# Second GEMM half a batch behind the first, in a Nystrom-attention and squared-ReLU kernel

## Chip, cores, metric

One core of a Trainium2 chip. The metric is device time in microseconds (us) of one execution, median of several. A ratio is the mean time of one kernel's fast runs over the mean of the other's in the same rounds, so it is not quite the ratio of the medians quoted. On one core, executions come in a state "fast" unless they are over 1.5% above the fastest of the same kernel.

Names: PE is TensorE (PEld its weight loads), DVE is VectorE, ACT is ScalarE, POOL is GpSimd, SP is SyncE. A "q" behind a name means its instruction queue, as in SPq.

## The reference, cut

```python
# B, H, S, D = 8, 8, 576, 64;  m = 32 landmarks;  d_model 512, d_ff 2048
q_lm, k_lm = segment means of q and k            # 32 segments of 18 rows
A, Bm, C = softmax(q k_lm^T/8), softmax(q_lm k_lm^T/8), softmax(q_lm k^T/8)
Z = Bm^T / (norm1(Bm) * norminf(Bm) + 1e-6)
for _ in range(6): Z = 2*Z - Z @ Bm @ Z          # Newton steps
x = (A @ Z @ C @ v) as [4608, 512]
h = relu(x @ w_in);  out = (h*h) @ w_out         # first GEMM, second GEMM
```

## The kernel before: what the argument touches

The eight batches run as a software pipeline: while batch b goes through the first GEMM, attention of batch b+1 is interleaved, and the second GEMM works on batch b-1. A list scheduler reorders instructions of each engine by priority, so the program order is a wish, not the final order. Each engine then executes its own queue in order.

Loads come in through GpSimd's queue and are cast to bf16. Tails are the last 64 rows of q and k:

```python
def load_qk(b, X):
    X["qkt"] = loads.tile([P, H, D], BF16, tag="qkt", name="qkt")
    for nm, src, r0 in (("k", k, TAIL), ("q", q, 0)):
        raw = loads.tile([P, H, NC4, D], BF16, tag="raw", name="raw")
        nc.gpsimd.dma_start(raw[:], ...)                       # bulk of k, then of q
        nc.gpsimd.dma_start(X["qkt"][r0:r0 + TAIL, :, :], ...) # its tail
```

VectorE then copies each into another layout, and from batch 2 on a transposing DMA issued by SyncE makes the transposed form:

```python
def prepare(b):
    for nm in ("k", "q"):
        X[nm] = loads.tile(..., tag=nm + "nat", bufs=1, name="nat")
        nc.vector.tensor_copy(X[nm][:], X[nm + "raw"]...)      # waits for the load
        if b >= 2:
            nc.sync.dma_start_transpose(X[nm + "T"]..., X[nm]...)
```

First GEMM, second GEMM and the loop:

```python
def mlp_in(b, f, AT, G, gT):           # 16 f-blocks a batch
    h = psum.tile([P, 2, 512], F32, tag="h", bufs=2, name="h")
    ... 4 matmuls of 288 columns
    nc.scalar.activation(r..., h[:, :, 0:HALF], AF.Relu)
    nc.vector.tensor_tensor(gT[:, f, o:o + S], r[:], r[:], ALU.mult)

def mlp_out(b, gT):                    # 9 tiles in two batches, 16 matmuls each
    for t in ...:
        ops = psum.tile([P, DM], F32, tag="o", bufs=1, name="ops")
        ... 16 matmuls of 512 columns, a yield after each
        o_sb = mlp.tile([P, DM], F32, tag="o", name="o_sb")    # two buffers
        if t % 2: nc.scalar.copy(o_sb[:], ops)
        else:     nc.vector.tensor_copy(o_sb[:], ops)
        nc.sync.dma_start(out_rows, o_sb[:])                   # store by SyncE

for b in range(B):
    load_qk(b + 2, ...); load_v(b + 2, ...)
    att, tiles = attention(b + 1, R), mlp_out(b - 1, prev)
    for u in range(2 * NF):
        if u % 2 == 0: mlp_in(b, u // 2, AT, G, gT)
        else:          advance(tiles, per)
        advance(att, ...)
        if u == NF and b + 2 < B: prepare(b + 2)
    ...
```

The softmax here doesn't subtract the row's maximum and nothing guards it: scores larger than these inputs give would overflow.

## Time and profile before

Median 315.67 us (315.25 to 315.75, 4 runs).

The view of the stages, kernel before: for each stretch of time its length, then the busy time of each engine in it with the number of instructions, the granted TensorE clock, the DMA share and what DMA moved.

```profile
0.00:40.00 40.00, 20.87 (x262) 15.20 (x263) 23.15 (x67) 12.96 (x30) 22.10 (x39) 0.83 1.28 176
40.00:60.00 20.00, 16.08 (x163) 11.92 (x162) 13.31 (x37) 13.86 (x26) 3.81 (x5) 0.83 1.52 163
60.00:80.00 20.00, 13.55 (x145) 7.62 (x144) 13.69 (x32) 6.58 (x13) 4.68 (x6) 0.88 1.44 170
80.00:100.00 20.00, 18.98 (x174) 12.15 (x172) 16.53 (x41) 12.59 (x26) 1.56 (x2) 0.95 1.01 129
100.00:180.00 80.00, 78.17 (x753) 45.26 (x752) 58.28 (x134) 44.08 (x82) 13.13 (x16) 1.00 0.85 121
```

The first busy figure is TensorE's. From 100 us on it is busy 98% of the time; the idle time lies in the first 100 us.

The waits of TensorE from 38 to 104 us, kernel before (who waited for whom, total us, times, longest us), the three longest:

```profile
PE h L419 <- DVE G L410: 5.4, 2, 5.1
PE n L353 <- DVE st L242: 3.8, 1, 3.8
PE n L368 <- ACT U L356: 0.8, 2, 0.5
```

Two waits make up nearly all of it, and both are for VectorE. The waits of VectorE from 38 to 80 us, kernel before, say what VectorE stood at:

```profile
DVE nat L156 <- DMA T<-nat: 5.1, 1, 5.1
DVE nat L156 <- DMA raw<-in_k_dram: 3.8, 1, 3.8
```

And VectorE's instructions in order of time around both, kernel before (start, us, instruction, in brackets the idle time ahead of it and what ended it):

```profile
48.69 0.69 DVE L156 COPY nat<-raw 128x2048 bf16<-128x2048 bf16 x1 [3.83 <-DMA raw<-in_k_dram]
49.30 0.75 DVE L242 TENSOR_TENSOR st<-BS,blk 128x256 bf16<-128x256 f32 x2
...
75.03 0.70 DVE L156 COPY nat<-raw 128x2048 bf16<-128x2048 bf16 x1 [5.09 <-DMA T<-nat]
75.76 1.23 DVE L410 CAST G<-g 128x1024 bf16<-128x1024 f32 x1
```

Read it like this: at 44.9 us VectorE reached the copy of a coming batch's k whose load had not landed. Behind it in the queue stood the start of batch 1's Newton steps (line 242), which had all its inputs. The Trainium skill, "PSUM — Partial Sum Buffer", section "Engine vs sequencer instructions", says that these queues are strict FIFO; this trace agrees, at 3.83 and 5.09 us each. The second time the copy waited until the transposing DMA had read its single buffer.

**A measure used below.** Busy time hides small gaps and the clock, so I also count work: each weight load in a stretch stands for one matmul, and each kind gets its spacing back to back as this trace shows it (216 ns in the second GEMM, 122 ns in the first, 25 to 134 ns for the small ones). The stretch less that sum is "lost time". It is an estimate. Its level hangs on the spacings taken for the small matmuls, so read only the differences between kernels; they are good to about 1 us a stretch.

### The profile page before, as it was taken

The page shows a single profiled execution, that of the slowest core. Times are in us where ns is not written, and L with a number is a line of the kernel's source. Part 1 is how long each engine was busy: PE and PEld are TensorE (multiplying, and loading weights), DVE is VectorE, ACT ScalarE, POOL GpSimd, SP SyncE. Part 2 cuts the span into 40 slices and gives each one's busy share as a digit, 9 for nine tenths or more (in the row PEclk, how much of TensorE's full clock was granted, in tenths as well). Part 3 has the DMA queues.
Part 4 walks back from the last instruction along what each step waited for, and adds up shares of the span by engine and source line. Part 5 has one row for each costly group of instructions (what it writes and reads, how often), then busy time and mean ns, then how long its engine had stood idle before and what let it go on. Part 6 is the DMA issues. An engine that isn't in the chain of part 4 may idle for free.

```text
span 315.4 us, 6319 instructions
## 1 busy us (share of the span) xinstructions
PE 276.1 (88%) x2536; PEld 164.8 (52%) x2536; DVE 201.4 (64%) x473; ACT 154.3 (49%) x291; POOL 46.9 (15%) x70
## 2 busy tenths in 40 slices
PE   0376786983998999999999999999989999999994
PEld 0264455642664566555655566466635665555441
DVE  3358765984797577768785858677964686544010
ACT  1053474731764466446744574448534754555000
POOL 8733513121010300104010401000000000000000
PEclk9995695997799999999999999999999999999999
DMA  8999999999967399819982996563000101000131
GB/s 90 186 198 201 203 198 167 127 174 168 176 87 110 88 124 176 125 70 142 154 143 72 138 144 148 82 123 83 33 35 34 35 35 67 33 35 33 67 102 67
DMA packets 75358, 35.28 MB, mean 112 GB/s; under 512 B 42049, under 2 KB 70721, under 8 KB 75329
## 3 DMA queue, kind: packets, MB, share of 16 engines
q0 software_dynamic: 41856, 18.35, 48.5%
q1 hardware_dynamic: 33472, 16.52, 27.8%
q8 instruction: 20, 0.33, 0.5%
q14 instruction: 10, 0.07, 0.1%
HBM read 36.70 MB, written 9.44 MB: 146 GB/s over the span
## 4 chain that ended last, share of the span: by engine, by line
PE 63%; DMA 18%; DVE 8%; ACT 5%; issue 4%; POOL 2%; DVEq 0%; POOLq 0%; ACTq 0%
PE ops L435 31%; PE h L419 15%; DMA T<-nat 6%; DMA w_in_bf<-in_moe_w_in_dram 5%; DMA raw<-in_k_dram 4%; DMA vm<-in_v_dram 3%; ACT r L423 3%; PE g L402 2%; PE n L279 2%; PE n L329 2%; PE n L353 2%; DVE gT L424 2%; PE n L368 1%; DVE ra L306 1%; PE n L177 1%
## 5 line engine op out<-in xcount | busy, mean ns | idle before, releaser
L435 PE MATMUL ops<-w_out_bf,gT 128*128 128x512 bf16 x544 | 145.4, 380 | 3.3 <-DVE o_sb L443 1.6
L423 ACT ACTIVATE r<-h 128x576 bf16<-128x576 f32 x128 | 82.9, 654 | 69.0 <-PE h L419 53.2
L419 PE MATMUL h<-AT,G 128*128 128x288 bf16 x512 | 87.4, 294 | 6.0 <-DVE G L410 5.4
L424 DVE TENSOR_TENSOR gT<-r 128x576 bf16<-128x576 bf16 x128 | 57.0, 449 | 40.3 <-ACT r L423 39.8
L435 PEld LDWEIGHTS <-gT 128*128 128x128 bf16 x576 | 51.7, 98 | 44.9 <-issue 7.5
L419 PEld LDWEIGHTS <-G 128*128 128x128 bf16 x512 | 48.0, 100 | 27.4 <-issue 8.4
L356 ACT CAST U<-n 128x256 bf16<-128x256 f32 (+1 forms) x54 | 18.7, 353 | 20.6 <-PE n L353 20.4
L408 ACT CAST G<-g 128x1024 bf16<-128x1024 f32 x16 | 16.2, 1012 | 21.9 <-PE g L402 21.8
L443 DVE COPY o_sb<-ops 128x512 f32<-128x512 f32 x20 | 13.7, 685 | 20.2 <-PE ops L435 20.2
L410 DVE CAST G<-g 128x1024 bf16<-128x1024 f32 x16 | 19.6, 1225 | 10.8 <-PE g L402 10.7
L156 DVE COPY nat<-raw 128x2048 bf16<-128x2048 bf16 x16 | 11.2, 700 | 17.9 <-DMA raw<-in_k_dram 7.7
L370 DVE SCALAR_TENSOR_TENSOR st<-st,n 128x256 bf16<-128x256 bf16 (+1 forms) x45 | 17.0, 386 | 8.2 <-PE n L368 7.0
L353 PE MATMUL n<-st,BT 128*128 128x128 bf16 x96 | 14.4, 228 | 6.4 <-DVE st L242 3.8
L177 PE MATMUL n<-seg,nat 128*128 128x32 bf16 x256 | 11.3, 180 | 8.4 <-DVE nat L156 8.4
L375 DVE STREAM_TRANSPOSE st<-st 128x256 bf16<-128x256 bf16 (+1 forms) x45 | 17.8, 402 | 0.6
L84 POOL DMA_DIRECT2D vm<-in_v_dram x8 | 7.1, 884 | 71.1 <-PE n L331 69.5
L353 PEld LDWEIGHTS <-BT 128*128 128x128 bf16 x96 | 8.8, 101 | 16.0 <-DVE st L242 4.3
L177 PEld LDWEIGHTS <-nat 128*128 128x128 bf16 x256 | 10.3, 98 | 11.7 <-DVE nat L156 8.6
L73 POOL DMA_DIRECT2D raw<-in_k_dram x8 | 8.0, 1003 | 55.8 <-DVE nat L156 55.0
L279 PEld LDWEIGHTS <-T 128*128 128x128 bf16 x256 | 12.0, 102 | 2.9 <-issue 2.2
L402 PE MATMUL g<-w_in_bf,WT 64*32 64x512 bf16 x256 | 12.4, 412 | 0.7 <-ACT G L408 0.5
L306 DVE TENSOR_REDUCE ra<-EA 128x40 f32<-128x1280 f32 x8 | 11.8, 1475 | 1.4 <-ACT EA L295 1.1
(153 smaller groups left out, 307.1 us busy)
## 6 DMA issues: line engine op xcount, KB each, us to landing
out_dram<-o_sb SPq DMA_DIRECT2D x32, 256.0 KB, 2.4
raw<-in_k_dram POOLq DMA_DIRECT2D x8, 512.0 KB, 11.9
raw<-in_q_dram POOLq DMA_DIRECT2D x8, 512.0 KB, 14.1
vm<-in_v_dram POOLq DMA_DIRECT2D x8, 512.0 KB, 8.1
w_in_bf<-in_moe_w_in_dram POOLq DMA_DIRECT2D x4, 512.0 KB, 12.7
w_out_bf<-in_moe_w_out_dram POOLq DMA_DIRECT2D x4, 512.0 KB, 16.8
out_dram<-o_sb SPq DMA_DIRECT2D x8, 128.0 KB, 6.0
qkt<-in_k_dram POOLq DMA_DIRECT2D x8, 64.0 KB, 12.3
```

The source lines that it names most:

```text
L177: nc.tensor.matmul(means[:, ti, p, :], lhsT=src.rearrange("p h d -> p (h d)"), rhs=seg[:, c + (ti if c == NC4 else 0), :], start=(c == 0), ...
L279: nc.tensor.matmul(sc[:, :, c, j, :] if nm == "q" else sc[:, c, j, :, :], lhsT=X[nm + "T"][:, c, p, :], rhs=BD[:, 1 if nm == "q" else 0, p ...
L353: nc.tensor.matmul(nu[:, qd - g[0], :], lhsT=BT[:, qd, :], rhs=st[:, 0, qd, :], start=True, stop=True)
L356: nc.scalar.copy(Ug[:], nu[:])
L370: last = nc.vector.scalar_tensor_tensor(out=res[:, g[0]:g[-1] + 1, :].rearrange("p q n -> p (q n)"), in0=st[:, z, g[0]:g[-1] + 1, :].rearr ...
L375: nc.vector.transpose(stn[:, 1, g[0]:g[-1] + 1, :].rearrange("p q n -> p (q n)"), stn[:, 0, g[0]:g[-1] + 1, :].rearrange("p q n -> p (q n)"))
L402: nc.tensor.matmul(g[M * p:M * p + M, i, :], lhsT=WT[64 * i:64 * i + 64, p, M * i:M * i + M], rhs=w_in_bf[64 * i:64 * i + 64, p, n * 512:n ...
L410: nc.vector.tensor_copy(dst, g[:])
L419: nc.tensor.matmul(h[:, j, 0:HALF], lhsT=G[:, qd, f * P:(f + 1) * P], rhs=AT[:, qd, j * HALF:(j + 1) * HALF], start=(qd == 0), stop=(qd == 1))
L423: nc.scalar.activation(r.rearrange("p (j t) -> p j t", j=2), h[:, :, 0:HALF], AF.Relu)
L424: nc.vector.tensor_tensor(gT[:, f, o:o + S], r[:], r[:], ALU.mult)
L435: nc.tensor.matmul(ops, lhsT=gT[:, f, t * P:t * P + P], rhs=w_out_bf[:, f, :], start=(f == 0), stop=(f == NF - 1))
```

## The change

Its intent: fill the early stages, in which TensorE has little to do but attention's latency chain, with the second GEMM of the same batch; keep VectorE from standing at copies whose data are not there; shorten batch 0's attention, which nothing overlaps; and take outputs off VectorE and SyncE. The core of the diff, cuts marked:

```diff
+DMA_T = 3                                   # transposing DMA only from batch 3 on
 ... load order: w_in 0, 1, then v of batch 0, w_in 2, 3, then q/k of batch 1, w_out, v of batch 1
-            if b >= 2:
+            if b >= DMA_T:
                 nc.sync.dma_start_transpose(...)
 ... attention of batch 0: prepare(0, ("k",)) and k's means and transposes first, then q;
     transposes in the "h" PSUM; fixed VectorE order; one group instead of two
 ... all batches: BT ahead of the scaling, Newton step 0 from BT; row sums of A in halves;
     the scaling of C v and one copy of A^T on ScalarE; g blocks 2, 3 behind the last output matmul
+            if it == (5 if b < 2 else 1):
+                X["pin"] = last             # this Newton step's update on VectorE
 def mlp_out(b, gT):
-            if b == B - 1 and t % 2:
+            if t % NC4 == 0 and t < 8 or b == B - 1 and t % 2 == 0:
                 ops = psum.tile([P, 2, DM], F32, tag="h", ...)   # the first GEMM's PSUM
-            o_sb = mlp.tile([P, DM], F32, tag="o", name="o_sb")
-            if t % 2: nc.scalar.copy(...)  else: nc.vector.tensor_copy(...)
+            o_sb = mlp.tile([P, DM], F32, tag="o", bufs=3, name="o_sb")
+            nc.scalar.copy(o_sb[:], ops)
-                nc.sync.dma_start(rows[:, c, :], o_sb[:])
+                nc.scalar.dma_start(rows[:, c, :], o_sb[:])
 loop over b:
-        tiles = mlp_out(b - 1, prev)        # in turn with all of mlp_in(b)
-            if u == NF and b + 2 < B: prepare(b + 2)
+        for f in range(NF):
+            mlp_in(b, f, AT, G, gT)
+            advance(tiles, 3 if b % 2 == 0 else 2)
+            attend(...)                     # 60% of attention(b + 1)
+        tiles = mlp_out(b, gT)              # of the same batch
+        for u in range(8):
+            advance(tiles, 3)
+            attend(...)                     # the other 40%
+ in attend, once "pin" of batch b + 1 exists:
+            with tc.issue_after(loaded[b + 1]["pin"].ins): prepare(b + 2)
```

More of the change, by code (lines that the diff above doesn't have):

```diff
@@ L1 @@
-from contextlib import ExitStack
+from contextlib import ExitStack, nullcontext
 import concourse.bass as bass
@@ L115 @@
     nc.vector.memset(ones_bf[:], 1.0)
-    load_v(0, loaded[0])
     def load_w_in(j):
@@ L126 @@
     load_w_in(1)
+    load_v(0, loaded[0])
+    load_w_in(2)
+    load_w_in(3)
     bds = []
@@ L137 @@
     load_qk(1, loaded[1])
-    load_w_in(2)
-    load_w_in(3)
-    load_v(1, loaded[1])
     for j in range(4):
@@ L145, with prepare @@
         )
+    load_v(1, loaded[1])
     def ntile(shape, dt=F32):
         return psum.tile(shape, dt, tag="n", bufs=3, name="n")
-    def prepare(b: int):
+    def prepare(b: int, nms=("k", "q")):
         X = loaded[b]
-        for nm in ("k", "q"):
+        for nm in nms:
             X[nm] = loads.tile([P, NC4, H, D], BF16, tag=nm + "nat", bufs=1, name="nat")
@@ L160, in prepare, with transposes @@
                     X[nm].rearrange("p c h d -> p (c h d)"))
-        X["tT"] = attn.tile([P, NPAIR, P], BF16, tag="tT", name="tT")
-        if b >= 2:
-            nc.sync.dma_start_transpose(X["tT"][:], X["qkt"].rearrange("p h d -> p (h d)"))
+        if "q" in nms:
+            X["tT"] = attn.tile([P, NPAIR, P], BF16, tag="tT", name="tT")
+            if b >= DMA_T:
+                nc.sync.dma_start_transpose(X["tT"][:], X["qkt"].rearrange("p h d -> p (h d)"))
     def attention(b: int, R: dict):
-        X = loaded.pop(b)
+        X = loaded[b]
         BD = bds[b % 2]
         ect = ects[b % 2]
-        groups = [(0,), (1,)] if b == 0 else [(0, 1)]
+        first = b == 0
+        def transposes(nm, half):
+            if first:
+                tps = psum.tile([P, 2, 2, NPAIR, P], BF16, tag="h", bufs=2, name="tps")[:, 0, :, :, :]
+            else:
+                tps = ntile([P, 2, NPAIR, P], BF16)[:]
+            for i in range(2):
+                for p in range(NPAIR):
+                    nc.tensor.transpose(
+                        tps[:, i, p, :],
+                        X[nm][:, 2 * half + i, 2 * p:2 * p + 2, :].rearrange("p h d -> p (h d)"),
+                        ident_bf[:],
+                    )
+            dst = X[nm + "T"][:, 2 * half:2 * half + 2, :, :]
+            if half == 0 and not (first and nm == "q"):
+                nc.vector.tensor_copy(dst, tps)
+            else:
+                nc.scalar.copy(dst, tps)
         means = ntile([P, 2, NPAIR, M])
+        STk = small.tile([P, NPAIR, M], BF16, tag="STk", name="STk")
         for ti, nm in ((1, "k"), (0, "q")):
+            if first:
+                prepare(0, (nm,))
             for p in range(NPAIR):
@@ L182, in attention @@
                     )
-            yield
-        STk = small.tile([P, NPAIR, M], BF16, tag="STk", name="STk")
-        nc.scalar.copy(STk[:], means[:, 1, :, :])
-        nc.scalar.copy(BD[0:64, :, :, 0:M], means[0:64, :, :, :])
-        nc.vector.tensor_copy(BD[64:128, :, :, M:2 * M], means[64:128, :, :, :])
-        def transposes(nm, half):
-            tps = ntile([P, 2, NPAIR, P], BF16)
-            for i in range(2):
-                for p in range(NPAIR):
-                    nc.tensor.transpose(
-                        tps[:, i, p, :],
-                        X[nm][:, 2 * half + i, 2 * p:2 * p + 2, :].rearrange("p h d -> p (h d)"),
-                        ident_bf[:],
-                    )
-            dst = X[nm + "T"][:, 2 * half:2 * half + 2, :, :]
-            if half == 0:
-                nc.vector.tensor_copy(dst, tps[:])
-            else:
-                nc.scalar.copy(dst, tps[:])
+            lo = nc.scalar.copy(BD[0:64, ti, :, 0:M], means[0:64, ti, :, :])
+            hi = nc.vector.tensor_copy(BD[64:128, ti, :, M:2 * M], means[64:128, ti, :, :])
+            tc.declare_no_dep(hi.ins, lo.ins, reason="other partitions")
+            if nm == "k":
+                nc.scalar.copy(STk[:], means[:, 1, :, :])
+                if first:
+                    transposes("k", 0)
+                    transposes("k", 1)
+            yield
         bm = ntile([P, 2, M])
@@ L222, in attention @@
         yield
-        if b < 2:
+        if b < DMA_T:
             transposes("q", 0)
@@ L235, in attention @@
         nc.vector.reciprocal(rc[:], c1[:])
-        BS = small.tile([P, 2, 2, M], F32, tag="BS", name="BS")
-        nc.vector.tensor_tensor(
-            BS[:], BB[:],
-            rc[:, :].unsqueeze(1).unsqueeze(3).to_broadcast([P, 2, 2, M]), ALU.mult)
         def spread(dst, src):
@@ L246, in attention @@
         spread(BT[:], BB[:, 0, :, :])
+        BS = small.tile([P, 2, 2, M], F32, tag="BS", name="BS")
+        nc.vector.tensor_tensor(
+            BS[:], BB[:],
+            rc[:, :].unsqueeze(1).unsqueeze(3).to_broadcast([P, 2, 2, M]), ALU.mult)
         st = newt.tile([P, 2, 2, 4, M], BF16, tag="st", name="st")
-        for z in range(2):
+        for z in (1, 0):
             spread(st[:, z, :, :, :], BS[:, z, :, :])
@@ L252, in attention @@
         yield
-        if b < 2:
+        if b < DMA_T:
             for nm, half in (("q", 1), ("k", 0), ("k", 1)):
-                transposes(nm, half)
-                yield
+                if not first or nm == "q":
+                    transposes(nm, half)
+                    yield
             tps = ntile([P, NPAIR, P], BF16)
@@ L300, in tails, with a_sums, a_rows, a_transposed @@
                 tl[P - TAIL:P, :, 0, :], AF.Exp, scale=SCALE)
-        def a_rows():
-            ea = EA.rearrange("p q c (h m) -> p (q c h) m", m=M)
-            n = 2 * (NC4 + 1) * 4
-            ra = small.tile([P, n], F32, tag="ra", name="ra")
-            nc.vector.reduce_sum(ra[:], ea, axis=AX.X)
-            rra = small.tile([P, n], F32, tag="rra", name="rra")
-            nc.vector.reciprocal(rra[:], ra[:])
-            nc.vector.tensor_tensor(an.rearrange("p q c (h m) -> p (q c h) m", m=M), ea,
-                                    rra[:, :].unsqueeze(2).to_broadcast([P, n, M]), ALU.mult)
-        def a_transposed(qd):
+        rra = [None, None]
+        def a_sums(i):
+            ra = small.tile([P, (NC4 + 1) * 4], F32, tag="ra", name="ra")
+            nc.vector.reduce_sum(ra[:], EA[:, i, :, :].rearrange("p c (h m) -> p (c h) m", m=M),
+                                 axis=AX.X)
+            rra[i] = small.tile([P, (NC4 + 1) * 4], F32, tag="rra", name="rra")
+            nc.vector.reciprocal(rra[i][:], ra[:])
+        def a_rows(i):
+            nc.vector.tensor_tensor(
+                an[:, i, :, :].rearrange("p c (h m) -> p (c h) m", m=M),
+                EA[:, i, :, :].rearrange("p c (h m) -> p (c h) m", m=M),
+                rra[i][:, :].unsqueeze(2).to_broadcast([P, (NC4 + 1) * 4, M]), ALU.mult)
+        def a_transposed(i):
             tps = ntile([P, (NC4 + 1) * P], BF16)
@@ L316, in a_transposed @@
                 o = j * P - (TAIL if b % 2 and j else 0)
-                nc.tensor.transpose(tps[:, o:o + P], an[:, qd, c, :], ident_bf[:])
-            nc.vector.tensor_copy(AT[:, qd, :], tps[:, 0:S])
+                nc.tensor.transpose(tps[:, o:o + P], an[:, i, c, :], ident_bf[:])
+            if i == 0 and not first:
+                nc.vector.tensor_copy(AT[:, i, :], tps[:, 0:S])
+            else:
+                nc.scalar.copy(AT[:, i, :], tps[:, 0:S])
         cvbs = [None, None]
@@ L335, in c_values @@
             cvb = small.tile([P, 4 * D], BF16, tag="cvb", name="cvb")
-            nc.vector.tensor_scalar(out=cvb[:], in0=cv[:, 0:4 * D], scalar1=rc2[:], scalar2=None,
-                                    op0=ALU.mult)
+            nc.scalar.activation(cvb[:], cv[:, 0:4 * D], AF.Copy, scale=rc2[:])
             cvbs[qd] = cvb
-        side = [lambda: scores("q", 0), lambda: scores("q", 1), lambda: scores("k", 0),
-                lambda: scores("k", 1), tails, a_rows, lambda: c_values(0),
-                lambda: c_values(1), lambda: a_transposed(0), lambda: a_transposed(1)]
@@ L345, in attention, with aside @@
-        zt = None
+        side = [(scores, "q", 0), (scores, "q", 1), (tails,), (a_sums, 0, scores, "k", 0),
+                (a_rows, 0, scores, "k", 1), (a_sums, 1, a_transposed, 0),
+                (a_rows, 1, c_values, 0), (a_transposed, 1), (c_values, 1)]
+        def aside():
+            f, *args = side.pop(0)
+            if f in (a_sums, a_rows):
+                f(args[0])
+                f, *args = args[1:]
+            f(*args)
         zt = newt.tile([P, 2, P], BF16, tag="zt", name="zt")
-        U = [None, None]
@@ L348, in attention @@
         for it in range(6):
-            stn = newt.tile([P, 2, 2, P], BF16, tag="st", name="st")
-            for g in groups:
-                nu = ntile([P, len(g), P])
-                for qd in g:
-                    nc.tensor.matmul(nu[:, qd - g[0], :], lhsT=BT[:, qd, :], rhs=st[:, 0, qd, :],
-                                     start=True, stop=True)
-                Ug = newt.tile([P, len(g), P], BF16, tag="U", name="U")
-                nc.scalar.copy(Ug[:], nu[:])
-                for qd in g:
-                    U[qd] = Ug[:, qd - g[0], :]
+            nu = ntile([P, 2, P])
@@ new lines, in attention @@
+            for qd in range(2):
+                nc.tensor.matmul(nu[:, qd, :], lhsT=BT[:, qd, :],
+                                 rhs=st[:, 0, qd, :] if it else BT[:, qd, :],
+                                 start=True, stop=True)
+            U = newt.tile([P, 2, P], BF16, tag="U", name="U")
+            if it:
+                nc.scalar.copy(U[:], nu[:])
+            else:
+                for qd in range(2):
+                    nc.scalar.activation(U[:, qd, :], nu[:, qd, :], AF.Copy, scale=rc[:, qd:qd + 1])
@@ L359, in attention @@
             yield
             if side:
-                side.pop(0)()
+                aside()
                 yield
-            for g in groups:
-                nv = ntile([P, len(g), P])
-                z = 0 if it < 5 else 1
-                for qd in g:
-                    a, c = (st[:, 1, qd, :], U[qd]) if it < 5 else (U[qd], st[:, 1, qd, :])
-                    nc.tensor.matmul(nv[:, qd - g[0], :], lhsT=a, rhs=c, start=True, stop=True)
-                res = stn[:, 0, :, :] if it < 5 else zt[:]
-                last = nc.vector.scalar_tensor_tensor(
-                    out=res[:, g[0]:g[-1] + 1, :].rearrange("p q n -> p (q n)"),
-                    in0=st[:, z, g[0]:g[-1] + 1, :].rearrange("p q n -> p (q n)"), scalar=2.0,
-                    in1=nv.rearrange("p q n -> p (q n)"), op0=ALU.mult, op1=ALU.subtract)
-                if it < 5:
-                    nc.vector.transpose(
-                        stn[:, 1, g[0]:g[-1] + 1, :].rearrange("p q n -> p (q n)"),
-                        stn[:, 0, g[0]:g[-1] + 1, :].rearrange("p q n -> p (q n)"))
@@ L378, in attention @@
-            st = stn
-            if it == 5:
-                X["last"] = last
+            nv = ntile([P, 2, P])
+            for qd in range(2):
+                x, y = (st[:, 1, qd, :], U[:, qd, :]) if it < 5 else (U[:, qd, :], st[:, 1, qd, :])
+                nc.tensor.matmul(nv[:, qd, :], lhsT=x, rhs=y, start=True, stop=True)
+            if it < 5:
+                stn = newt.tile([P, 2, 2, P], BF16, tag="st", name="st")
+                res, old = stn[:, 0, :, :], st[:, 0, :, :]
+            else:
+                res, old = zt[:], st[:, 1, :, :]
@@ L381, in attention @@
+            last = nc.vector.scalar_tensor_tensor(out=res, in0=old, scalar=2.0, in1=nv[:],
+                                                  op0=ALU.mult, op1=ALU.subtract)
+            if it < 5:
+                nc.vector.transpose(stn[:, 1, :, :].rearrange("p q n -> p (q n)"),
+                                    stn[:, 0, :, :].rearrange("p q n -> p (q n)"))
+                st = stn
+            if it == (5 if b < 2 else 1):
+                X["pin"] = last
             yield
             if side:
-                side.pop(0)()
+                aside()
@@ L398, in attention @@
         for n in range(4):
-            g = psum.tile([P, 2, 512], F32, tag="h", bufs=2, name="g")
-            for p in range(NPAIR):
-                for i in range(2):
-                    nc.tensor.matmul(g[M * p:M * p + M, i, :],
-                                     lhsT=WT[64 * i:64 * i + 64, p, M * i:M * i + M],
-                                     rhs=w_in_bf[64 * i:64 * i + 64, p, n * 512:n * 512 + 512],
-                                     start=True, stop=True)
+            with tc.issue_after(mark[0].ins) if n == 2 and mark else nullcontext():
+                g = psum.tile([P, 2, 512], F32, tag="h", bufs=2, name="g")
+                for p in range(NPAIR):
+                    for i in range(2):
+                        nc.tensor.matmul(g[M * p:M * p + M, i, :],
+                                         lhsT=WT[64 * i:64 * i + 64, p, M * i:M * i + M],
+                                         rhs=w_in_bf[64 * i:64 * i + 64, p, n * 512:n * 512 + 512],
+                                         start=True, stop=True)
             dst = G[:, :, n * 512:n * 512 + 512]
@@ L411, in attention @@
                 yield
-        R[b] = (AT, G, X["last"])
+        R[b] = (AT, G)
+    mark = []
     def mlp_in(b, f, AT, G, gT):
@@ L434, in mlp_out @@
             for f in range(NF):
-                nc.tensor.matmul(ops, lhsT=gT[:, f, t * P:t * P + P], rhs=w_out_bf[:, f, :],
-                                 start=(f == 0), stop=(f == NF - 1))
+                mark[:] = [nc.tensor.matmul(ops, lhsT=gT[:, f, t * P:t * P + P], rhs=w_out_bf[:, f, :],
+                                            start=(f == 0), stop=(f == NF - 1))]
                 if f < NF - 1:
                     yield
-            o_sb = mlp.tile([P, DM], F32, tag="o", name="o_sb")
-            if t % 2:
-                nc.scalar.copy(o_sb[:], ops)
-            else:
-                nc.vector.tensor_copy(o_sb[:], ops)
+            o_sb = mlp.tile([P, DM], F32, tag="o", bufs=3, name="o_sb")
+            nc.scalar.copy(o_sb[:], ops)
             if t == NC4:
@@ L446, in mlp_out @@
                     r0 = (b0 + i) * S + NC4 * P
-                    nc.sync.dma_start(out[r0:r0 + TAIL, :], o_sb[64 * i:64 * i + TAIL, :])
+                    nc.scalar.dma_start(out[r0:r0 + TAIL, :], o_sb[64 * i:64 * i + TAIL, :])
             else:
@@ L460 @@
     R = {}
-    prepare(0)
-    for _ in attention(0, R):
-        pass
-    with tc.issue_after(R[0][2].ins):
+    with tc.manual_schedule(engines={mybir.EngineType.DVE}):
+        for _ in attention(0, R):
+            pass
+    with tc.issue_after(loaded[0]["pin"].ins):
         prepare(1)
-    gT, prev = None, None
+    gT, tiles = None, iter(())
     for b in range(B):
@@ L472, with attend @@
             gT = mlp.tile([P, NF, 2 * S], BF16, tag="gT", name="gT")
-        AT, G, _ = R.pop(b)
+        AT, G = R.pop(b)
         att = attention(b + 1, R) if b + 1 < B else iter(())
-        tiles = mlp_out(b - 1, prev) if b else iter(())
-        per = (4 if b % 2 == 0 else 3) if b else 0
+        steps = 31 if b + 1 < DMA_T else 26
+        half = steps * 6 // 10
         done = 0
-        for u in range(2 * NF):
-            if u % 2 == 0:
-                mlp_in(b, u // 2, AT, G, gT)
-            else:
-                advance(tiles, per)
-            want = (u + 1) * (31 if b == 0 else 26) // (2 * NF)
-            advance(att, want - done)
-            if u == NF and b + 2 < B:
-                prepare(b + 2)
-            done = want
-        while advance(att, 1):
-            advance(tiles, 4)
+        def attend(want):
+            nonlocal done
+            while done < want:
+                advance(att, 1)
+                done += 1
+                if b + 2 < B and "pin" in loaded[b + 1] and "q" not in loaded[b + 2]:
+                    with tc.issue_after(loaded[b + 1]["pin"].ins):
+                        prepare(b + 2)
+        for f in range(NF):
+            mlp_in(b, f, AT, G, gT)
+            advance(tiles, 3 if b % 2 == 0 else 2)
+            attend((f + 1) * half // NF)
         for _ in tiles:
             pass
-        prev = gT
-    for _ in mlp_out(B - 1, prev):
+        tiles = mlp_out(b, gT)
+        for u in range(8):
+            advance(tiles, 3)
+            attend(half + (u + 1) * (steps - half) // 8)
+        while b + 1 not in R and b + 1 < B:
+            advance(tiles, 6)
+            attend(done + 1)
+    for _ in tiles:
         pass
```

## The prediction

> **What bounds the kernel now.** In the stage windows TensorE is busy 195.7 of 200 us between 100 and 300 us, at a granted clock of 1.00. Back to back, one second-GEMM matmul takes 216 ns (16 in 3.45 us in the final chain) and one first-GEMM matmul 122 ns. All matmuls at such spacings make, as an estimate, 257 us of TensorE work; about 58 of the 315 us are lost. By stretches: 28 us before the first first-GEMM matmul (38.3 us), 20 us from there to 104 us, only about 6 in the steady state, 4.4 after the last matmul. The gain must come from the first 100 us.
>
> Losses there (waits of TensorE): 3.8 us at 46 us, because VectorE, in order, sits at the copy of batch 2's k, whose load lands at 48.6 us, with batch 1's Newton start queued behind; 5.1 us at 72 us, because the next such copy waits for the transposing DMA (18.8 us to landing) and the G copy is queued behind. After such a gap first-GEMM matmuls run at 240 ns (granted clock 0.76): the Trainium skill, "TensorE: Matmul & The Clock Gate", Part 1, says an idle window halves the clock, and this trace agrees. Then thin filling: while batch 1's attention runs its latency chain (39 to 66 us), only 24 second-GEMM matmuls run before 77 us.
>
> **What the change does.**
> 1. Copies pinned behind a Newton step, batch 2 transposed on TensorE: both VectorE blockages go, 8.9 us plus 2 to 4 us of cold clock.
> 2. Batch 0's attention: k's means and transposes move into the wait for q (8.3 to 11.6 us); step 0 starts from BT; one group instead of two; half-size row sums. Newton now runs 19.5 to 33.6 us, 2.35 us a step, against about 1.6 us for the bare chain of matmul, U copy, matmul, update. First first-GEMM matmul 38.3 -> about 33.5 us: -5.
> 3. Second GEMM of the same batch as filler early: -4 to -6.
> 4. Costs: 36 transposes on TensorE for batch 2 and five PSUM copies: +2 to 3 us. ScalarE takes 20 more output copies (0.585 us each, 11.7 us) and 40 DMA issues (0.33 us each on SyncE, 13 us), plus waits for its own copies. It goes from 154 to about 175 us busy plus issue, under 70%: off the critical path, but relu and U copies sit behind it, so +1 to +4 us in the steady state.
>
> **Sum:** 315.6 - 11.5 - 5 - 5 + 2.5 + 2.5 = 299, rounded to 300 us. 8 in 10: 290 to 309. Faster by over 2%: 0.86; within: 0.11; slower: 0.03.
>
> **What would show each step.** (1) No TensorE wait over 3 us after 30 us; clock 1.00 from about 60 us. (2) First first-GEMM matmul near 33.5 us. (3) Batch 1's first-GEMM stage starts near 61 us instead of 77, with over 30 second-GEMM matmuls before it. (4) Steady batches stay at 31.0 us; TensorE's waits on ScalarE (r, U) rise by some us at most; ScalarE busy about 175 us.
>
> **What would make it wrong.** Loads: v of batch 0 now comes behind two weight pieces, q/k of batch 1 behind four; if they land later than about 22 and 29 us, attention stalls and the start gains nothing. PSUM buffers shared by output tiles and first GEMM could make the first GEMM wait for an output copy. ScalarE blocked at each store could delay relu and idle TensorE once per tile (36 x 0.3 us would take back 10 us). In the other direction, if the early stages fill completely, 290 us.

## The result

Median 300.58 us (299.68 to 300.68, 4 runs) against 315.67; ratio of fast runs 0.9518, 95% interval 0.9498 to 0.9538. The profiled executions span 315.4 and 299.0 us.

The stages of the kernel after, the same stretches as above:

```profile
0.00:40.00 40.00, 21.23 (x254) 15.57 (x255) 20.90 (x54) 15.25 (x31) 21.61 (x39) 1.00 1.26 178
40.00:60.00 20.00, 19.33 (x191) 13.79 (x192) 16.65 (x46) 15.13 (x32) 2.56 (x4) 1.00 1.15 136
60.00:80.00 20.00, 18.99 (x209) 11.92 (x211) 14.13 (x35) 12.90 (x24) 3.33 (x4) 1.00 0.80 123
80.00:100.00 20.00, 18.90 (x183) 11.60 (x184) 14.05 (x33) 13.34 (x29) 4.69 (x6) 1.00 0.84 126
100.00:180.00 80.00, 77.50 (x758) 47.08 (x769) 54.11 (x134) 53.72 (x106) 11.17 (x14) 1.00 0.96 129
```

TensorE's busy time rose in the stretches from 40 to 80 us, from 29.6 to 38.3 us, and not in the first. The waits of TensorE from 38 to 104 us, kernel after, the three longest; nothing is left of the two long ones:

```profile
PE ops L461 <- ACT o_sb L466: 0.5, 2, 0.3
PE h L445 <- ACT G L432: 0.5, 1, 0.5
PE n L390 <- ACT U L379: 0.5, 1, 0.5
```

Lost time in us by stretch (the estimate explained above); the last column is the stretch to the end of the span. Experiments that are told further down are in the same table:

| kernel | 0-40 | 40-60 | 60-80 | 80-100 | 100-290 | rest |
|---|---|---|---|---|---|---|
| before | 28.2 | 7.0 | 9.3 | 3.1 | 11.1 | 4.7 |
| after | 28.8 | 2.6 | 1.1 | 1.5 | 7.4 | 4.5 |
| e1 (before, pin) | 28.7 | 2.9 | 3.4 | 4.5 | 24.1 | 4.3 |
| e9 (e1, five buffers) | 29.1 | 3.1 | 4.1 | 2.1 | 11.1 | 4.4 |
| e12 (before, three parts) | 28.7 | 3.2 | 0.8 | 0.9 | 7.4 | 4.4 |
| e3 (after, old order) | 28.7 | 3.0 | 5.1 | 2.8 | 7.0 | 4.2 |
| e6 (after, old outputs) | 28.6 | 2.4 | 1.5 | 1.8 | 12.9 | 4.5 |
| e7 (after, tails first) | 27.0 | 1.7 | 1.2 | 1.4 | 6.2 | 4.5 |

So the gain lies between 40 and 100 us (19.4 lost before, 5.2 after: 14.2 us) and in the steady state, the stretch from 100 to 290 us (3.7 us); the start gave nothing. The 36 added transposes are 2 us more work (36 x 56 ns).

### The profile page after: what moved, and what is told of

Same layout as the page of the kernel before. It is cut to its first block, busy times and chain, and to the rows that moved or that the text cites. A ratio compares the mean times of both kernels' runs of the same rounds, so it can differ in the third digit from the quotient of the medians.

```text
span 299.0 us, 6321 instructions
## 1 busy us (share of the span) xinstructions
PE 268.0 (90%) x2532; PEld 165.4 (55%) x2572; DVE 184.2 (62%) x451; ACT 180.2 (60%) x349; POOL 46.9 (16%) x70
## 4 chain that ended last, share of the span: by engine, by line
PE 70%; DVE 11%; ACT 10%; issue 4%; DMA 3%; POOL 1%; ACTq 0%; POOLq 0%
PE ops L461 26%; PE h L445 16%; PE n L348 3%; PE n L199 3%; DMA qkt<-in_q_dram 3%; PE g L426 3%; ACT r L449 3%; ACT o_sb L466 2%; ACT G L432 2%; DVE gT L450 2%; PE n L390 2%; PE n L333 2%; PE n L374 2%; ACT EA L295 1%; DVE ra L317 1%
## 5 line engine op out<-in xcount | busy, mean ns | idle before, releaser
L461 PE MATMUL ops<-w_out_bf,gT 128*128 128x512 bf16 x383 | 108.1, 379 | 4.0 <-ACT o_sb L466 1.6
L445 PE MATMUL h<-AT,G 128*128 128x288 bf16 x512 | 85.2, 289 | 1.0 <-ACT G L432 0.5
L450 DVE TENSOR_TENSOR gT<-r 128x576 bf16<-128x576 bf16 x128 | 57.6, 453 | 39.4 <-ACT r L449 38.3
L445 PEld LDWEIGHTS <-G 128*128 128x128 bf16 x512 | 46.7, 99 | 20.0 <-issue 3.8
L466 ACT COPY o_sb<-ops 128x512 f32<-128x512 f32 x26 | 15.2, 586 | 12.7 <-PE ops L461 12.7
L379 ACT CAST U<-n 128x256 bf16<-128x256 f32 x40 | 15.2, 380 | 11.5 <-PE n L374 10.7
L396 DVE SCALAR_TENSOR_TENSOR st<-st,n 128x256 bf16<-128x256 bf16 x40 | 16.6, 414 | 5.8 <-PE n L390 5.1
L199 PE MATMUL n<-seg,nat 128*128 128x32 bf16 x256 | 10.6, 180 | 8.8 <-DVE nat L156 8.8
L399 DVE STREAM_TRANSPOSE st<-st 128x256 bf16<-128x256 bf16 x40 | 17.5, 438 | 0.6
L199 PEld LDWEIGHTS <-nat 128*128 128x128 bf16 x256 | 10.1, 98 | 13.0 <-DVE nat L156 9.2
L290 PEld LDWEIGHTS <-T 128*128 128x128 bf16 x256 | 13.0, 102 | 4.5 <-issue 0.6
L156 DVE COPY nat<-raw 128x2048 bf16<-128x2048 bf16 x16 | 11.1, 699 | 3.9 <-DMA raw<-in_k_dram 3.9
L77 POOL DMA_DIRECT2D qkt<-in_k_dram x8 | 5.5, 690 | 47.7 <-PE n L199 18.9
L323 DVE TENSOR_TENSOR an<-EA,rra 128x640 bf16<-128x640 f32 x16 | 12.9, 809 | 0.1
## 6 DMA issues: line engine op xcount, KB each, us to landing
vm<-in_v_dram POOLq DMA_DIRECT2D x8, 512.0 KB, 13.5
w_in_bf<-in_moe_w_in_dram POOLq DMA_DIRECT2D x4, 512.0 KB, 11.1
```

Source lines behind the costliest of these rows:

```text
L199: nc.tensor.matmul(means[:, ti, p, :], lhsT=src.rearrange("p h d -> p (h d)"), rhs=seg[:, c + (ti if c == NC4 else 0), :], start=(c == 0), ...
L379: nc.scalar.copy(U[:], nu[:])
L396: last = nc.vector.scalar_tensor_tensor(out=res, in0=old, scalar=2.0, in1=nv[:], op0=ALU.mult, op1=ALU.subtract)
L399: nc.vector.transpose(stn[:, 1, :, :].rearrange("p q n -> p (q n)"), stn[:, 0, :, :].rearrange("p q n -> p (q n)"))
L445: nc.tensor.matmul(h[:, j, 0:HALF], lhsT=G[:, qd, f * P:(f + 1) * P], rhs=AT[:, qd, j * HALF:(j + 1) * HALF], start=(qd == 0), stop=(qd == 1))
L461: mark[:] = [nc.tensor.matmul(ops, lhsT=gT[:, f, t * P:t * P + P], rhs=w_out_bf[:, f, :], start=(f == 0), stop=(f == NF - 1))]
```

## The experiments

Twelve kernels ran, all with correct results, timed beside the kernel before on the same chip. Most were not timed beside the kernel after: a difference to after is one of medians from different rounds, in which before itself moved by 0.6 us. Summary first (medians, us; before in those rounds was 315.4 to 316.0):

| run | what | us | ratio to before, 95% |
|---|---|---|---|
| e1 | before + pinned copies, batch 2 on TensorE | 323.41 | 1.024 (1.022 to 1.027) |
| e2 | before + new order of the GEMMs | 318.41 | 1.012 (1.007 to 1.016) |
| e3 | after, old order of the GEMMs | 306.24 | 0.971 (0.969 to 0.973) |
| e4 | after, copies not pinned | 304.79 | 0.967 (0.965 to 0.968) |
| e5 | after, batch 2 by transposing DMA | 310.33 | 0.983 (0.979 to 0.987) |
| e6 | after, outputs as before | 306.34 | 0.969 (0.965 to 0.972) |
| e7 | after, q's tail loaded before q's bulk | 298.18 | 0.944 (0.941 to 0.947) |
| e8 | after, batch 0 built like the others | 300.01 | 0.950 (0.947 to 0.953) |
| e9 | e1 with five output buffers | 308.11 | 0.976 (0.974 to 0.979) |
| e12 | before + pin + order + outputs | 300.23 | 0.951 (0.949 to 0.954) |
| e10 | e7, side work of batch 0 spread | 296.69 | 0.939 (0.936 to 0.941) |
| e11 | e10, more in batch 0 | 296.45 | 0.939 (0.937 to 0.941) |

My first theory (A) was that VectorE's blocked queue was the main cause; the rival (B), that filling early stages with the second GEMM was. Both expected that one of the two parts, put alone on the kernel before, brings most of the gain.

### e1: the pin alone, on the kernel before

```diff
+DMA_T = 3                     # and b >= 2, b < 2 become b >= DMA_T, b < DMA_T
+            if it == (5 if b < 2 else 1): X["pin"] = last
-            if u == NF and b + 2 < B: prepare(b + 2)
+  after each step of attention(b + 1), once it has its pin:
+            with tc.issue_after(loaded[b + 1]["pin"].ins): prepare(b + 2)
```

> The kernel before with only the pinned copies and batch 2 transposed on TensorE; order of the GEMMs, start, outputs as before. Theory A (VectorE blocked behind copies that wait for DMA is the main cause): 304 to 307 us, and no TensorE wait over 2 us after 30 us. Theory B (the gain is filler: the second GEMM of the same batch fills the early latency chain): 312 to 315 us, because TensorE waits elsewhere in the same chain.

Measured: 323.41 us, slower than before. Both theories fall as stated. The blockages of VectorE are gone (after 20 us its trace shows no wait for a load or a transposing DMA at these copies), yet TensorE waits elsewhere. Its waits from 110 us on, e1, the longest:

```profile
PE ops L438 <- ACT o_sb L444: 9.8, 4, 4.5
```

With one wait before that (2.2 us) this is 12.0 us. The waits of ScalarE over the whole run, e1, say why ScalarE was late:

```profile
ACT o_sb L444 <- DMA out_dram<-o_sb: 13.5, 4, 4.2
```

ScalarE stood at an output copy because the output buffer was still being stored. SyncE's queue (line 159 the transposing DMA, line 454 a store) and the two output copies of ScalarE (line 444) around the first such case, e1, in order of time:

```profile
79.63 7.29 SPq L159 DMA_TRANSPOSE T<-nat  x1
86.97 1.42 SPq L454 DMA_DIRECT2D out_dram<-o_sb  x1
```

```profile
79.74 0.58 ACT L444 COPY o_sb<-ops 128x512 f32<-128x512 f32 x1
97.17 0.59 ACT L444 COPY o_sb<-ops 128x512 f32<-128x512 f32 x1 [3.40 <-DMA out_dram<-o_sb]
```

The output tile was in its buffer at 80.3 us; SyncE was occupied with issuing a transposing DMA until 86.9 us and could issue the store only then; the store landed at 97.1 us, and the copy that needed the buffer again ran at 97.2 us. The transposing DMA is the second of a pair: the first, issued at 77.4 us, held SyncE for only 2.2 us. Matching output copies to stores in order of time, six stores of e1 were issued over 1 us after their data were ready (up to 8.0 us), against three (up to 4.2 us) in the kernel before. So pinning removed one blocked queue and made another, through the store, with two output buffers between them. The relu of the first GEMM stands behind that copy in ScalarE's queue as well.

### e9: e1 with five output buffers

```diff
-            o_sb = mlp.tile([P, DM], F32, tag="o", name="o_sb")
+            o_sb = mlp.tile([P, DM], F32, tag="o", bufs=5, name="o_sb")
```

> e1 (the kernel before with pinned copies and batch 2 on TensorE, 323 us) with five output buffers instead of two; nothing else. Theory Q (e1 is slow because stores, issued by SyncE in order behind the transposing DMAs, free the two output buffers late, so that ScalarE stands at an output copy and TensorE behind it for 12 us in 5 waits): those waits go, 309 to 313 us. Rival (the pinned order itself is bad with the old order of the GEMMs): 320 us or more.

Measured: 308.11 us, 15.3 us under e1 and 7.8 us under before, a little better than expected. TensorE's longest wait for an output copy after 110 us is now 0.5 us, and no wait for a store is left at ScalarE's copies:

```profile
PE ops L438 <- DVE o_sb L446: 1.1, 2, 0.5
PE ops L438 <- ACT o_sb L444: 1.1, 3, 0.4
```

The cause is shown: late-freed output buffers cost e1 its gain. The stores did not get earlier (six are again issued late, by up to 8.4 us); the three more buffers keep the lateness from reaching an engine. Lateness has two parts, the issue behind the transposing DMA (6.7 us in the case above) and the landing of the store (2.0 to 10.1 us in e1). What each costs alone was not tested; buffers cure both.

### e2: the order alone, on the kernel before

```diff
 the loop of the change, with prepare(b + 2) in the middle of the first GEMM and not pinned
```

> The kernel before with only the new order of the GEMMs (second GEMM half a batch behind); copies not pinned, batch 2 by transposing DMA. Theory A: 312 to 316 us, the two TensorE waits of 3.8 and 5.1 us (VectorE copy) still there. Theory B: 303 to 308 us, the waits being filled with second-GEMM matmuls.

Measured: 318.41 us, 1.2% slower than before. VectorE's blocked copy is still there, now at q's load, and costs TensorE 5.9 us in one wait; the second, the wait for the transposing DMA, does not occur in this trace. But lost time from 100 to 290 us is 18.2 us against 11.1. The profiled execution was the slowest of the four (321.25 us; the others took 318.2 to 318.5), so up to 3 us of this may belong to that execution. TensorE waits there in many small pieces for the Newton updates (4.0 us in 5 waits after 104 us); no wait for a store appears. Which of the parts it lacks would cure that (single output bank, output copies on VectorE, the unpinned copies), this run does not say; e12 shows that together they do.

### e3 and e4: one part taken out of the change

e3 restores the old loop (tiles of batch b-1 in turn with mlp_in(b)), copies still pinned. e4:

```diff
-                if b + 2 < B and "pin" in loaded[b + 1] and "q" not in loaded[b + 2]:
-                    with tc.issue_after(loaded[b + 1]["pin"].ins): prepare(b + 2)
+            if f == NF // 2 and b + 2 < B: prepare(b + 2)
```

> The kernel after with only the order of the GEMMs undone. Theory A: 302 to 305 us (order worth 2 to 4). Theory B: 308 to 312 us, most of the gain gone.

> The kernel after with the copies of coming q/k placed in the middle of the first GEMM again and not pinned; batch 2 still transposed on TensorE. Theory A: 305 to 311 us, VectorE waits of several us at the copy for its load come back. Theory B: 300 to 303 us.

Measured: e3 306.24 (5.7 us over after), e4 304.79 (4.2 over). Neither theory's numbers fit both (A comes nearer: e4 lies 0.2 us under its range, e3 1.2 us over): each part is worth 4 to 6 us when the rest is present. In e3 no single wait is long; lost time from 60 to 100 us is 7.9 us against 2.6, the thin filling that the prediction named. Before the first GEMM of batch 1 starts, 16 second-GEMM matmuls have been issued in e3, 43 in after (counted by weight loads). In e4 VectorE stands at a copy again. Its longest wait from 30 to 70 us, e4:

```profile
DVE nat L156 <- DMA raw<-in_q_dram: 5.4, 1, 5.4
```

TensorE waits 5.3 us behind it. It happens once, not twice. That batch 2 no longer uses the transposing DMA is not shown to be the reason: in e2, where it does, the second wait is missing too.

### e5: batch 2 by transposing DMA again

```diff
-DMA_T = 3
+DMA_T = 2
```

> The kernel after with batch 2 transposed by DMA again, copies still pinned. If the transposing DMA of batch 2 competes with the early loads and holds a copy on VectorE: +2 to +5 us. If the pin alone is enough, TensorE saves 36 transposes (2 us of work): -1 to -2 us.

Measured: 310.33 us, 9.7 us over after, twice the upper end expected. The mechanism is not the expected one: no copy is held, TensorE itself waits for the transposed k. Its wait, e5, up to 110 us:

```profile
PE n L290 <- DMA T<-nat: 8.6, 1, 8.6
```

The pin sets this: for batch 2 the copy may start only after batch 1's last Newton step, and the DMA's result is needed right after (the copies ran at 64.3 us, straight behind that step; the second of the two transposing DMAs landed at 86.4 us, when TensorE went on). With the pin, 36 transposes on TensorE (2 us) buy off a wait of 8.6 us.

### e6: outputs as before

```diff
-            nc.scalar.copy(o_sb[:], ops)
+            if t % 2: nc.scalar.copy(o_sb[:], ops)
+            else:     nc.vector.tensor_copy(o_sb[:], ops)
-                nc.scalar.dma_start(...)
+                nc.sync.dma_start(...)
```

> The kernel after with output copies on VectorE and ScalarE in turn and stores by SyncE, as before. If moving outputs to ScalarE relieves VectorE and is part of the steady gain (4.5 us): +1 to +3 us. If it costs because ScalarE blocks at its stores, as the prediction allowed: -1 to -3 us. If it is off the critical path: within 0.5 us.

Measured: 306.34 us, 5.8 us over after, though this kernel has three output buffers, and more than any of the three cases expected. The line-by-line views of the output copies, e6, show the same kind of wait as in e1, once on each engine (after the bar: busy us, mean ns, then idle us before them and what ended it):

```profile
L469 DVE COPY o_sb<-ops 128x512 f32<-128x512 f32 x20 | 13.6, 679 | 18.4 <-PE ops L461 15.5 <-DMA out_dram<-o_sb 2.9
L467 ACT COPY o_sb<-ops 128x512 f32<-128x512 f32 x16 | 9.4, 588 | 16.9 <-PE ops L461 11.2 <-DMA out_dram<-o_sb 5.7
```

Seven stores are issued late again (by up to 8.3 us), none by over 1 us in after. A store's landing is not what the move cures: in after, too, the 14 stores issued while a transposing DMA was in flight landed after 3.4 to 10.6 us, the other 26 after 2.3 us in median. What the prediction booked as a cost (ScalarE takes all outputs and issues their stores) is worth 5.8 us. TensorE's waits for output copies after 100 us explain 3.0 us of it (4.1 us against 1.1). The edit moves copies and stores together, so a part may be relief of VectorE; that was not tested apart. Five of its six runs lay between 306.0 and 307.2 us, one at 303.7.

### e8 and e7: why the start gave nothing

e8 builds batch 0 like the others (`first = False`, both copies ahead, no fixed VectorE order).

> The kernel after with batch 0's attention built like the other batches (both copies first, means of k and q together in the n banks, transposes after the row sums, no fixed VectorE order). If the special start is worth nothing, as the equal 38.3 us of before and after suggest: within 1 us of after. If it is worth the predicted 5 us and something else in the change took it back (load order): +4 to +5 us.

Measured: 300.01 us, the same as after. The special start is worth nothing with loads in this order. Why shows in TensorE's first instructions. Before (line 177 are means, line 193 transposes, line 419 the first GEMM), cut:

```profile
11.62 0.19 PE L177 MATMUL n<-seg,qkt 128*128 128x32 bf16 x1 [3.23 <-DMA qkt<-in_q_dram]
...
13.95 1.01 PE L193 MATMUL n<-ident_bf,nat 128*128 128x128 bf16 x8
...
38.29 0.65 PE L419 MATMUL h<-AT,G 128*128 128x288 bf16 x4 [0.41 <-ACT G L408]
```

After (line 199 means, line 180 transposes, line 445 the first GEMM), cut:

```profile
11.86 0.19 PE L199 MATMUL n<-seg,qkt 128*128 128x32 bf16 x1 [3.51 <-DMA qkt<-in_q_dram]
...
12.28 1.87 PE L180 MATMUL tps<-ident_bf,nat 128*128 128x128 bf16 x16
14.68 0.29 PE L199 MATMUL n<-seg,nat 128*128 128x32 bf16 x4 [0.53 <-DVE nat L156]
...
38.29 1.12 PE L445 MATMUL h<-AT,G 128*128 128x288 bf16 x4 [0.49 <-ACT G L432]
```

The fifth matmul of k's means reads the tile that holds the tails of both q and k, and q's tail is the last piece of the load. TensorE therefore stood at its fifth matmul until q was complete, in both kernels, and k's transposes, behind it in the queue, did not move into the wait. They now came after it and pushed q's copy and means back by 2.7 us (12.0 to 14.7 us). e7 changes only the order of four loads, but in all eight batches:

```diff
-        k bulk, k tail, q bulk, q tail
+        k bulk, k tail, q tail, q bulk
```

> The kernel after with the load of q's tail issued straight after k's tail, ahead of the bulk of q; nothing else. Theory S (the start gained nothing because k's means need the tile that holds both tails, so TensorE waits for q's tail until 11.9 us and k's transposes do not move into the wait): TensorE goes on at about 8.5 to 9 us, Newton starts about 1.5 to 2 us earlier, first first-GEMM matmul at about 36.5 us instead of 38.3, time -1.5 to -2 us. Rival (the start is bound by something else, such as the Newton chain with its side work): first first-GEMM matmul still near 38 us, time within 0.5 us.

Measured: 298.18 us, 2.4 us under after, a little more than expected. TensorE, e7 (line 204 means, 185 transposes):

```profile
8.51 0.18 PE L204 MATMUL n<-seg,qkt 128*128 128x32 bf16 x1
...
8.94 1.87 PE L185 MATMUL tps<-ident_bf,nat 128*128 128x128 bf16 x16
12.09 0.29 PE L204 MATMUL n<-seg,nat 128*128 128x32 bf16 x4 [1.28 <-DVE nat L161]
```

The transposes of k now run inside the wait for q, as the change intended, and the first first-GEMM matmul comes at 35.7 us instead of 38.3. That moment differs from profile to profile: in e3 to e6, which have the start of after, it lies between 37.1 and 38.7 us, in e8 at 36.7. So the profiles alone would be thin evidence; the times of six runs each carry it. By the table some lost time also goes later (1.2 us from 100 to 290 us), so not all of the 2.4 us need be batch 0's.

### e12: the three parts together, on the kernel before

e1 plus the loop of the change plus its mlp_out (outputs by ScalarE, three buffers, two tiles in nine in the first GEMM's PSUM). Load order, start, row sums and copies inside attention stay as before.

> The kernel before with three parts of the change together: pinned copies with batch 2 on TensorE, the new order of the GEMMs, and outputs by ScalarE with three buffers and the first GEMM's PSUM; the old load order, start, row sums and copies in attention stay. If the gain is these three acting together, though two of them alone made it slower: 299 to 304 us. If the small pieces in attention or the load order are needed too: 306 us or more.

Measured: 300.23 us, the time of the whole change. So the gain is these three acting together: alone, the pin cost 8 us and the order 3 us (outputs alone were not run); together they gain 15. Two at a time, with the rest of the change, gain 9 to 11 us: e3 has pin and outputs, e4 order and outputs, e6 pin and order with a third buffer. The rest of the change (about half of the diff) adds nothing that these runs can tell from zero.

### e10 and e11: further in the start

e10 keeps e7 and, in batch 0, allots one piece of side work to each Newton step:

```diff
+        if first:
+            side = [(scores, "q", 0), (scores, "q", 1), (tails,), (a_sums, 0, scores, "k", 0),
+                    (scores, "k", 1), (a_rows, 0, c_part, 0, 0), (c_part, 0, 1),
+                    (a_sums, 1, c_part, 1, 0), (c_part, 1, 1), (a_rows, 1), (a_transposed, 0),
+                    (a_transposed, 1)]          # c_part: c_values in two parts
```

> e7 (298.2 us) with the side work of batch 0 spread over its Newton steps: one VectorE piece a step, the values' product in two parts, the transposes of A at the end. If the side work in VectorE's and TensorE's order is what makes a step 2.27 us instead of about 1.65: Newton of batch 0 takes 10.5 to 11.5 us instead of 13.6, the first first-GEMM matmul comes at about 33 us, time 295.5 to 296.5. If the start is bound by the loads of batch 1 by then, the time stays within 0.7 us of e7.

Measured: 296.69 us, 1.5 us under e7; the last Newton update starts at 29.2 us instead of 30.6. The Newton steps thus take about 1.5 us less instead of the 2 to 3 us expected, so side work was only part of the 2.27 us a step. e11 adds two edits: q's transposes in batch 0 are issued after the exp of the row sums, and ScalarE and VectorE each take half of every G copy there.

> e10 and, in batch 0, ScalarE does the row sums' exp ahead of q's transposed copies (0.85 us on the chain) and both engines share each G copy (0.7 us): another 1 to 1.5 us, 294 to 295.5 us, first first-GEMM matmul about 31.5 us.

Measured: 296.45 us, not to be told from e10 and above the range expected; the first first-GEMM matmul comes at 34.8 us (34.5 in e10), not near 31.5. The last Newton update does come 1.0 us earlier (28.2 us), but then VectorE's wait for batch 1's q begins, in the old pattern. VectorE, e11:

```profile
31.44 0.69 DVE L161 COPY nat<-raw 128x2048 bf16<-128x2048 bf16 x1 [1.50 <-DMA raw<-in_q_dram]
```

The G copies stand behind it. Here, in this trace, the start meets the rate of the loads. e10 is the fastest version that is clearly told from e7: 0.939 of before.

## Why the prediction was right, and where it was not

The predicted 300 us met 300.58, inside the range. Point by point:

1. **VectorE's blockages go (8.9 us plus cold clock): right in effect.** No wait of TensorE after 30 us exceeds 0.5 us in the stretch to 104 us. With item 3 it was to bring 16.5 us; lost time from 40 to 100 us fell by 14.2. But the prediction added items as if each stood alone. e1 has item 1 alone and is 8 us slower than before. The step that failed is "both VectorE blockages go, 8.9 us plus 2 to 4 us of cold clock" taken as a gain of its own: it turns into a wait for output buffers unless outputs leave by another queue (e6 against after, 5.8 us) or have more buffers (e9 against e1, 15.3 us).
2. **Start: "First first-GEMM matmul 38.3 -> about 33.5 us: -5": wrong.** It came at 38.3 us in both. The step assumed that k's means could finish without q. The trace of before already showed TensorE waiting for q's tail at its fifth matmul; I read it as a wait for q, which it was not meant to be. e7 gives 2.6 us of it back with one load moved. Nor did the Newton steps get near 1.6 us: from their first matmul to their last update they took 13.8 us before and 13.2 us after, 2.2 us a step.
3. **Filler: right in worth, wrong in the stage's time.** In after, 43 second-GEMM matmuls were issued before batch 1's first GEMM, in before 21 (over 30 predicted). That stage began at 68.9 us, not near 61: 5 of the 8 us are those that the start did not give, the rest is not explained. The 77 us that I gave for before was wrong, because there it began at 70.7 us and then stood until 77.0. e3 shows what the filler is worth with everything else present: 5.7 us.
4. **Costs: the transposes right (2 us); the steady state wrong in sign.** I allowed +1 to +4 us for ScalarE's extra work. ScalarE's busy time went from 154.3 to 180.2 us; with 40 issues of 0.34 us that makes about 194 us, against 175 predicted with issue. The prediction did not count the scaling of C v (7.6 us) and the copies of A^T (5.8 us) that the change also moves to ScalarE. And yet lost time in the steady state fell by 3.7 us. From batch 2's first GEMM to batch 7's, five batches, TensorE took 162.3 us instead of 167.1 (4.8 less); the 31.0 us a batch in the prediction was a misreading of equal slices. ScalarE never blocked at a store: the trace of after shows no wait of its copies for one, and an issue takes 0.34 us in median, 0.97 at most. e6 and e1 show the other side: outputs on SyncE share a queue with the transposing DMAs.

So the sum was right partly by luck, because two errors cancelled: 5 us that the start did not give, and about 6 us (2.5 allowed, 3.7 gained) in the steady state. The gain's mechanism is shown by e1, e9, e6, e3, e4 and e12. Not settled: why the new order alone (e2) loses 4 to 7 us in the steady state, and how e6's 5.8 us divide between the stores' queue and VectorE's relief.

On the clock: the Trainium skill, "TensorE: Matmul & The Clock Gate", Part 1, has a busy-or-idle gate that halves the clock. The matmul spacing agrees (eight first-GEMM matmuls in 2.08 us at 77 us before, 240 ns from start to start, against 122), and the granted clock there is 0.50; the 0.76 in the prediction is a mean from 70 to 80 us. The granted clock in the profile is less sure, as that page warns of such records: after says 1.00 for 0 to 40 us, while its first-GEMM matmuls at 39.8 us also take 240 ns.

## What to carry to other kernels

Before moving an instruction off a blocked queue, ask which queue its consequence lands in: here the moved copies also moved transposing DMAs, these held back more stores on the same queue, and two output buffers carried the delay to TensorE, so that a correct repair alone made the kernel slower. Test parts both ways, alone on the old kernel and taken out of the new one, since parts that gain beside one another can look harmful one by one. And when work is to move into a wait, check what the first instruction in that wait really reads: one shared tile for two tails undid the new start, and moving one load of 64 KB brought 2.4 us.

## What the Trainium skill lacked or had wrong

- "DMA: Bandwidth & Descriptors", section "Issuing engines are not separate DMA queues", says that issuing from several engines saves only the sequencer's issue time, "which is usually small relative to the DMA itself". Here one transposing DMA held SyncE for 7.29 of the 16.35 us to its landing (e1; it was the second of a pair, and the first held SyncE for 2.23 us), a store with its data ready at 80.3 us was issued at 86.97 us, and moving stores from SyncE to ScalarE is worth 5.8 us (e6 against after; copies moved with them).
- The same page, "Latency and other measured facts", gives 261 GB/s for transposing DMAs with a non-contiguous middle dimension, and more for contiguous ones. At 261 GB/s 512 KB would take 2.0 us (an estimate from the page's figure). In the kernel after, counted from the start of the issue, the eight beside loads landed after 7.7 to 19.0 us; the last two, issued when all loads had landed, after 4.4 and 5.0 us. A sentence that says how a transposing DMA fares beside a loaded queue is missing.
- No page says that a pair of strict FIFO queues with few buffers between them passes a delay on: ScalarE waited 13.5 us for stores in e1 and TensorE 12.0 us for ScalarE's output copies; with five buffers instead of two (e9) the first is gone and the second is down to 1.1 us.
